# Row scales of the layer norm for two row tiles at a time, and a new order of instructions, in a linear attention and SwiGLU kernel

## The chip, the cores and the metric

The kernel runs on one core of a Trainium2 chip. The metric is the time of one execution on the device in microseconds (us); smaller is better. Engines are named as the profile names them: PE (matmul), PEld (its weight loads), DVE, ACT, POOL, and SP, which here only issues DMAs.

## The reference, cut to what matters

Two kinds of block alternate, twice: linear attention with 32 heads of 16, then a gated MLP. Each reads a layer norm of the running rows and is added to them. There are 2048 rows of 512 numbers, in float32; the MLP's hidden size is 1792. The second attention and the second MLP use the same weights as the first.

```python
def _layernorm(x, axis=-1, eps=1e-5):
    m = jnp.mean(x, axis=axis, keepdims=True)
    v = jnp.var(x, axis=axis, keepdims=True)
    return (x - m) / jnp.sqrt(v + eps)
...
x = x + _A_ref(_layernorm(x, axis=-1), A_wqkv, A_wo)
x = x + _B_ref(_layernorm(x, axis=-1), B_w1, B_w3, B_w2)
x = x + _A_ref(_layernorm(x, axis=-1), A_wqkv, A_wo)
x = x + _B_ref(_layernorm(x, axis=-1), B_w1, B_w3, B_w2)
```

In the attention q and k go through phi(t) = t + 1 or exp(t), plus 1e-6. The sums over all rows of k times v and of k are formed, q is multiplied with the first and divided by its product with the second, and the result goes through wo. The MLP is silu(x w1) times (x w3), times w2.

## The kernel before, in words

The 2048 rows are 16 row tiles of 128, which stay in SBUF as `x_sb`. Every matmul operand is a pair of float16 parts, high and low, and a product is three passes (high by high, low by high, high by low), which `mm` (line 565) issues. In the second layer's keys and queries and in both MLPs, products of two by two blocks are made with seven block products in place of eight, so that many small adds, casts and subtractions (lines 444, 442, 460, 458, 468) surround the matmuls.

For the layer norm of an attention's input, `ln_moments` makes mean and variance of a tile on DVE (BN_STATS and BN_AGGR, lines 526 and 527), and `ln_scale` makes from them the row scale and the row bias on POOL, in four instructions (lines 534, 535, 537, 538): variance plus epsilon, its power of minus one half, minus the mean, and the product of these. `ln_stats(t0, n)` calls both for the n tiles from t0 on; `ln_scale` makes one set of four instructions whatever n is, on n columns. `normalise` (lines 547 and 549) then applies scale and bias to a tile. The MLP's layer norm has code of its own (lines 1458 to 1477), which works on four tiles at a time.

A row tile of keys takes this way in the first layer: statistics, `normalise`, a cast to the high part and a subtraction for the low part (lines 442 or 444, and 468), a transposing DMA (line 1227), twelve matmuls with the key weights (line 565), phi on ACT and DVE (lines 948, 949, 950, 959), a split into high and low (lines 450 and 1048), and the products of the tile with itself that form the sums (line 980). The key weights `wk_s` have to be scaled and split first: four maxima over the weights (line 352), one maximum over them (368), a small matmul (371), a second maximum (373), some arithmetic on single columns (374, 376, 360, 384, 395), four scalings (450, 452) and four subtractions (400).

The first three tiles do not wait for that. `first_tile` normalises them, PE transposes them in float32 (line 1326, four instructions a tile), ACT or DVE copies the result out of the bank (1338, 1340), and `whole_product` multiplies them in float32 with the weights as they were loaded (line 1349, four instructions a tile). A float32 matmul stands in the trace as two. `keep_busy` issues matmuls of a constant tile `ones16` (line 1895; the constant is set by line 268); their results are not used. 19 of them come ahead of everything else in the code, and four behind the first three tiles.

None of this fixes the order in which an engine runs its instructions. `pin_all` does, from the table `ORDER`: one list of places per engine, where place k is the k-th instruction of that engine in the order of the code. `CHOICE` is a string of letters that gives, for each cast, add, scaling or normalisation of which several engines are capable, the engine: V for DVE, P for POOL, A for ACT. `BANKS` gives the PSUM bank of each product. The framework adds the semaphores that the data need. An engine thus runs its list strictly in order, and an instruction that waits holds up all that stands behind it on that engine.

Of the kernel before, what the change touches and what calls it, by code (L numbers as in the profile page):

```python
# [20 lines left out]
NT, NC, NK, NF = S // P, S // 512, D // P, F // P  # L21
# [62 lines left out]
def kernel(  # L84
# [321 lines left out]
    def table_of(what, layer):  # L406
# [3 lines left out]
        "VAPAAPPPAAAAVAPPVAAAPVAAPVAAPPAVPPVAAPAPAVAAAPAPPVVPAPPAAPVAAPAVPPPAVVAPVAAVAVAVAPPAAVAAAVPP"  # L410
        "VVVAPAAAVAAVVAAVAAVVVVAPAVVVAVVAVAVVVPAPAVAPAVPPPAPAVPPVVVPVAVVVAPVAVVAVVPPVAVAVAAPVAPAVAAVV"
        "PPPAVAAAVPVVPPAVAPAVAPAPAPAAAAAPVVVVAVAAPVPPAAAAAAPAPAPAPPVPVAVAPAVAVAAAAAVPPVPVVPPAAPVVPAAV"
        "VAVAVPAPPVAVPPVVAVAVPVAVAAAAAVAVPVVVAVAVVVVVAVAAVAVAAVVVPPAVPVVVVPAVAAVVVVAAVAVVVVVAVAVAVPAP"
        "VVPPVVVVAAPVAAAPAVAVAVVVVVAVAAVVVVVVVAAPPPVAAAVAPPVVAPPVAAAPVPPPPAVAAVPPPAAPVPVAVAAPPAVVVVVV"
        "AAAVVAVVPPVAVVVVVVAVVPVAAVVAAAVPPPPVVVVPVAVAAAAVVVVVAPVVAAVPVAVVPVVAVVVAAPAPVVVPVAAAVVVVVAVA"
        "PAAAAVVVVVVVAAAPVPVVPVVVPVVAAVVAPVAVAPVPVVAVPVAVAAAVVAPVPPVAVPVAAVVVVVVVAVAAAVVAPVPPVAVVVVVV"
        "AAAVVVVVVAVVVVVAAVPPPVVVVAVPVAVAAVAPAAVVVVPPVVVVVPPVVAVAPAVPPAPPPVPAVAPAAAVPAPVVPVAVPVAPPVPV"
        "VVVVVVVAVVVVPVVVAAAVPAPPPPPAVPPAAAAAVVVVVAVVPPVAVAPAVVPAAAAVPAPVVPPVVPVPVPVAVAAAAVPVVVVVAPAV"
        "APPAVPAVVVPVAVAAAVVAVPVVVAVPPVAVAAPPPPPAPVAAVPVAVPPPPAAPPVPPAVAAAVAAAVPPVPPPPPAVAAAAAAAAVAAV"
        "VPVPPVAAAVAAAVVVVPVVPPVVAVAAVAAPPVPVVPPVAVVAVAAVAAPAAVPVVVVVAAAAAVAVAAAVAAAVAAVAPVVVVAAVAPVP"  # L420
        "VPPAVPAVVAAAPAVVVVAAAAVAVPAVAAAAVAPVVVVAAAVAPAVVPVVVAPPAPVAAVAPAVAAVVVVPAPVAAAAAVAVVVPAPVAVA"
        "AAAAVPVVVAVVAAVAVVVVVAVAAAVPPVVVVAVAPPPVPAAPVVPPVVVAVPVAAAAAVPPPPAVVAVVAAAPVPPVVVVVAAAAVVVVV"
        "VVVVAPVVVAAVVVAVPPVAVVPAAAAVVVVVVVVAAPVAAAVVVVVVVVVVAAAVVVVVVVVAAPPVVAAPPAAVPVPVAPVAAAAAVVVV"
        "VVVVAVVAAVPPVVVVVVPAAVAVVVVVVPVAVVAAAAVVVVVVVVAAVVAAAVVPVPVVVVAAAAAVPVVVVVAVAAVVPVVVAVVAAAVV"
        "VVPVVVVAVVAAPPVVPVVVVVAAAVAPVVVVVVAAAAVVVVVVVVVAAVVVVVVVVVAAVVAAVVVVVVVVVVAAAVVVVVVVAVAAAVAP"
        "PVVVVVAAAAAVPVVVVVAAVVAAAVVPVVVVVVAAAAVVVVVVVVAAAVAVAVVVPV"
# [91 lines left out]
    def ln_stats(t0, n):  # L518

        ln_moments(t0, n)  # L520
        ln_scale(t0, n)

    def ln_moments(t0, n):
        for t in range(t0, t0 + n):
            st = small("st", 6)
            nc.vector.bn_stats(st, x_sb[:, t, :])
            nc.vector.bn_aggr(mv_all[:, t, :], st)
# [436 lines left out]
    def attention(layer, ready, prep, before_gram):  # L964
# [24 lines left out]
        for t in range(NT):  # L989
# [919 lines left out]
    ln_stats(1, 1)  # L1909
# [9 lines left out]
    ln_stats(2, 1)  # L1919
# [32 lines left out]
def pin_all(nc, tc):  # L1952
# [5 lines left out]
    for engine, runs in ORDER.items():  # L1958
# [370 lines left out]
```

## Time and profile before

| | us |
|---|---|
| median of three runs | 1141.81 |
| lowest and highest | 1139.44, 1142.08 |
| profiled execution, its time | 1141.3 |
| profiled execution, its span | 1139.5 |
| PE busy in the span | 1125.7 (99%) |
| DVE busy | 974.0 (85%) |
| ACT busy | 595.8 (52%) |
| POOL busy | 390.6 (34%) |

Times in views of the profile count from the start of the span. [...] The group name `arena` stands for nearly everything that lies in SBUF, as it is one tile with many views; lines tell the groups apart. The engine DVE has two instructions for some lines (one reads an accumulator).

### The profile page before, as it was taken

The numbers are of one execution on the slowest core, as the hardware profiler recorded it, in microseconds if no ns is written. First come the engines' busy times: TensorE is split into PE (matmuls) and PEld (weight loads), VectorE is DVE, ScalarE is ACT, GpSimd is POOL, SyncE is SP. The second block draws the span as 40 slices with busy tenths as digits, with TensorE's granted clock in tenths as the row PEclk, the third lists the DMA queues.
The fourth block names the chain that finished last, engine by engine and source line by source line (L and its number), as shares of the span: only waits on it lengthen the run. The fifth ranks groups of instructions, "written<-read, shape, count | busy, mean of one in ns | idle before, by whom it ended". The sixth has DMA issues, their size and how long they took to land.

```text
span 1139.5 us, 22555 instructions
## 1 busy us (share of the span) xinstructions
PE 1125.7 (99%) x9075; PEld 889.3 (78%) x9075; DVE 974.0 (85%) x1705; ACT 595.8 (52%) x1051; POOL 390.6 (34%) x458
## 2 busy tenths in 40 slices
PE   9999999999999999999999999999999999999998
PEld 4445445888888888888876676678888888888887
DVE  7787999999999999898899779989788766777767
ACT  5588778874555245435467657766433233222421
POOL 5750467333550442325688212444300100100000
PEclk9999999999999999999999999999999999999999
DMA  9997467677555232412567646646543613002012
GB/s 279 276 273 252 117 137 196 157 236 225 183 187 230 84 149 103 158 66 70 145 162 208 154 135 186 111 83 172 161 114 130 244 57 122 2 1 75 10 38 93
DMA packets 174298, 164.66 MB, mean 145 GB/s; under 512 B 138864, under 2 KB 150256, under 8 KB 169328
## 3 DMA queue, kind: packets, MB, share of 16 engines
q1 hardware_dynamic: 174192, 163.21, 48.4%
q8 instruction: 71, 1.16, 0.4%
q14 instruction: 35, 0.29, 0.1%
HBM read 80.87 MB, written 48.50 MB: 114 GB/s over the span
## 4 chain that ended last, share of the span: by engine, by line
PE 85%; DVE 8%; DMA 3%; POOL 2%; issue 1%; ACT 1%; SPq 0%; POOLq 0%; DVEq 0%; ACTq 0%
PE bank L565 59%; PE bank L1602 18%; PE bank L980 6%; DVE arena L468 4%; DMA arena<-arena 2%; POOL arena L468 1%; DMA arena<-in_B_w_dram 1%; DVE arena L1560 1%; DVE arena L1650 1%; DVE arena L1510 1%; PE bank L1895 1%; DVE arena L444 1%; POOL rs_all L535 0%; PE bank L1349 0%; POOL arena L460 0%
## 5 line engine op out<-in xcount | busy, mean ns | idle before, releaser
L565 PE MATMUL bank<-arena 128*128 128x256 f16 (+2 forms) x6228 | 804.7, 285 | 8.2 <-DMA arena<-arena 6.7
L565 PEld LDWEIGHTS <-arena 128*128 128x128 f16 x6228 | 605.1, 98 | 169.8 <-DMA arena<-arena 8.8
L468 POOL TENSOR_TENSOR arena<-arena 128x256 f32<-128x256 f32 (+5 forms) x251 | 285.8, 1152 | 633.7 <-DVE arena L1510 158.1
L468 DVE TENSOR_TENSOR arena<-arena 128x256 f32<-128x256 f32 (+4 forms) x555 | 390.4, 730 | 17.6 <-ACT arena L442 6.7
L1602 PE MATMUL bank<-arena 128*128 128x256 f16 x2310 | 291.6, 273 | 0.0
L1602 PEld LDWEIGHTS <-arena 128*128 128x128 f16 x2310 | 226.0, 98 | 26.4 <-ACT arena L442 0.2
L1555 ACT ACTIVATE arena<-bank 128x512 f32<-128x512 f32 x168 | 99.6, 594 | 227.8 <-PE bank L565 189.0
L442 ACT ACTIVATE arena<-arena 128x512 f16<-128x512 f32 (+3 forms) x203 | 153.0, 771 | 66.1 <-DVE arena L468 32.9
L1560 DVE TENSOR_TENSOR arena<-arena,bank 128x512 f32<-128x512 f32 x168 | 113.9, 682 | 39.5 <-ACT arena L1555 22.7
L1650 DVE SCALAR_TENSOR_TENSOR arena<-bank,scalars,arena 128x256 f32<-128x256 f32 (+1 forms) x200 | 111.2, 584 | 25.4 <-PE bank L1602 16.9
L1509 ACT ACTIVATE arena<-arena,scalars 128x512 f32<-128x512 f32 (+1 forms) x112 | 74.4, 666 | 95.2 <-DVE arena L1560 78.8
L1510 DVE SCALAR_TENSOR_TENSOR arena<-arena,scalars 128x512 f32<-128x512 f32 (+1 forms) x112 | 79.6, 713 | 21.7 <-ACT arena L1509 21.2
L980 PE MATMUL bank<-arena 128*128 128x512 f16 (+1 forms) x384 | 91.5, 379 | 0.3 <-DVE arena L1048 0.3
L980 PEld LDWEIGHTS <-arena 128*128 128x128 f16 (+1 forms) x384 | 38.8, 101 | 35.8 <-issue 0.6
L444 DVE CAST arena<-arena 128x512 f16<-128x512 f32 (+2 forms) x82 | 50.5, 619 | 5.5 <-POOL arena L460 1.8
L444 POOL CAST arena<-arena 128x512 f16<-128x512 f32 (+2 forms) x31 | 23.3, 753 | 81.8 <-DVE arena L1089 28.3
L547 ACT ACTIVATE arena<-arena,nb_all,rs_all 128x512 f32<-128x512 f32 x42 | 33.6, 807 | 8.1 <-DVE arena L468 6.5
L1652 ACT ACTIVATE arena<-bank,scalars 128x256 f32<-128x256 f32 x40 | 18.7, 468 | 32.6 <-PE bank L1602 20.2
L458 ACT ACTIVATE arena<-arena,scalars 128x512 f32<-128x512 f32 (+3 forms) x33 | 31.4, 956 | 7.2 <-DMA arena<-in_B_w_dram 4.2
L1048 DVE SCALAR_TENSOR_TENSOR arena<-arena,scalars 128x512 f16<-128x512 f32 x32 | 26.7, 834 | 5.3 <-ACT arena L450 5.0
L1292 ACT ACTIVATE arena<-bank 128x256 f32<-128x256 f32 x51 | 18.9, 375 | 17.4 <-PE bank L565 17.2
L450 ACT ACTIVATE arena<-arena,scalars 128x512 f16<-128x512 f32 x27 | 19.4, 720 | 13.8 <-DVE arena L959 13.4
(117 smaller groups left out, 626.1 us busy)
## 6 DMA issues: line engine op xcount, KB each, us to landing
arena<-xb_d SPq DMA_DIRECT2D x12, 1792.0 KB, 7.0
xb_d<-arena SPq DMA_DIRECT2D x8, 1792.0 KB, 7.2
w_d<-arena SPq DMA_DIRECT2D x5, 1792.0 KB, 7.5
arena<-w_d SPq DMA_DIRECT2D x5, 1792.0 KB, 10.2
arena<-in_B_w_dram SPq DMA_DIRECT2D x8, 896.0 KB, 6.3
arena<-in_B_w_dram SPq DMA_DIRECT2D x28, 256.0 KB, 3.1
xt_d<-arena SPq DMA_DIRECT2D x8, 896.0 KB, 4.3
arena<-xt_d SPq DMA_DIRECT2D x8, 896.0 KB, 5.0
```

The source lines that it names most:

```text
L442: engine.activation(dst, src, AF.Copy)
L444: engine.tensor_copy(dst, src)
L468: choose().tensor_tensor(dst, a, b, op)
L547: engine.activation(dst, x, AF.Identity, scale=scale, bias=bias)
L565: nc.tensor.matmul(dst, lhs(a, k), rhs(b, k), start=first and k == 0 and i == 0, stop=last and k == n - 1 and i == len(PASSES) - 1, skip_g ...
L980: nc.tensor.matmul(gt[j][:n], nat[:, first : first + n], pk[:, b, :], start=t == 0 and i == 0, stop=t == NT - 1 and i == len(PASSES) - 1, ...
L1509: nc.scalar.activation(t, gate, AF.Silu, scale=info["u1"])
L1510: nc.vector.scalar_tensor_tensor(t, up, info["hid"], t, OP.mult, OP.mult)
L1555: engine.activation(dst, bank_, AF.Copy)
L1560: nc.vector.tensor_tensor(dst, dst, bank_, OP.add)
L1602: nc.tensor.matmul(po[:, i * HALF : (i + 1) * HALF], hs[:, a, qx, cs], w2[:, b, qw, :], start=g == ends[0] and i + a + b == 0, stop=g == e ...
L1650: nc.vector.scalar_tensor_tensor(dst, src, cb, to, OP.mult, OP.add)
```

## The change

In the first layer's keys, statistics were made for tile t+4 at each tile t; now they are made for tiles t+4 and t+5 at each even t. In the second layer it was one call for each tile (two at t = 0); now it is one call for two tiles at t = 0 and at each odd t. Ahead of the loop tiles 1 and 2 share one call. The calls of `ln_scale` go from 29 to 16, so that 52 instructions on POOL are left out; 13 of the 16 sets that are left are two columns wide, two are one wide and one is four wide. BN_STATS and BN_AGGR stay one per tile.

```diff
@@ stats() in attention()
                 if layer == 1:
                     if t == 0:
-                        ln_stats(4, 1)
-                        ln_stats(5, 1)
-                    elif t + 5 < NT:
-                        ln_stats(t + 5, 1)
-                elif t + 4 < NT:
-                    ln_stats(t + 4, 1)
+                        ln_stats(4, 2)
+                    elif t % 2 and t + 5 < NT:
+                        ln_stats(t + 5, 2)
+                elif t % 2 == 0 and t + 4 < NT:
+                    ln_stats(t + 4, 2)
@@ ahead of the first layer
     whole_product(0)
-    ln_stats(1, 1)
+    ln_stats(1, 2)
...
     for _ in scale_chain:
         pass
-    ln_stats(2, 1)
     keep_busy(4)
@@ ORDER (one line of the five lists)
-        "0-13 19-22 14-17 23-26 35 18 27-30 40-43 36 31-34 44-47 37 51-53 38-39 48-50 54-56 72-83 "
...
```

`CHOICE` is a new string too. Counted over the whole program, 78 instructions go from POOL to DVE and 46 from DVE to POOL, 41 from ACT to DVE and 24 from DVE to ACT, 19 from ACT to POOL and 17 from POOL to ACT. With the 52 that are left out, the lists of instructions change from 1675 to 1724 on DVE, from 1004 to 985 on ACT and from 463 to 381 on POOL; PE keeps its 9034 matmuls and SP its DMAs, in new orders. From about the middle of the second layer's keys to the end of its attention, PE's list is nearly that of before.

The three places below are all at the start of the program. In the new file the same code stands one line higher from line 1045 on and two lines higher at the end. On PE, before; line 1895 is a matmul of the constant tile, and there are 14 of them ahead of the first row of line 1326, four, one, and one in the gaps that follow; banks 65, 67 and 70 take the transposed tiles 0, 1 and 2, banks 66, 68 and 71 their products:

```order
L2325 UNCONDITIONAL_BRANCH
L1895 LDWEIGHTS ones_76
L1895 MATMUL bank_64<-ones_76 128x512
...
L1326 MATMUL bank_65<-arena 128x128 x4
...
L1349 MATMUL bank_66<-arena 128x512 x4
L371 MATMUL bank_69<-arena,scalars 128x128
...
L1326 MATMUL bank_67<-arena 128x128 x4
L1326 MATMUL bank_70<-arena 128x128 x4
...
L1349 MATMUL bank_68<-arena 128x512 x4
L1349 MATMUL bank_71<-arena 128x512 x4
```

And on PE now, with three matmuls of line 1894 ahead of line 371, then six, seven and four in the gaps:

```order
L2319 UNCONDITIONAL_BRANCH
L1325 MATMUL bank_65<-arena 128x128 x4
L1348 MATMUL bank_66<-arena 128x512 x4
L1894 LDWEIGHTS ones_76
L1894 MATMUL bank_64<-ones_76 128x512
...
L371 MATMUL bank_69<-arena,scalars 128x128
...
L1325 MATMUL bank_67<-arena 128x128 x4
...
L1325 MATMUL bank_70<-arena 128x128 x4
...
L1348 MATMUL bank_68<-arena 128x512 x4
L1348 MATMUL bank_71<-arena 128x512 x4
```

All 14 matmuls of the constant that stood ahead of the first tile now stand behind its product, and 20 of them stand between the products of tile 0 and tile 1.

On DVE, before, from the first instruction on; line 268 sets the constant tile, line 549 normalises tile 0, line 352 takes the maxima of the key weights:

```order
L268 MEMSET ones_76 128x128
L526 BN_STATS arena<-arena 128x6
L527 BN_AGGR mv_all<-arena 128x2
L549 TENSOR_SCALAR arena<-arena,rs_all,nb_all 128x512
...
L352 TENSOR_REDUCE arena<-arena 128x1 x3
...
L368 TENSOR_REDUCE scalars<-arena 128x1
...
L373 TENSOR_REDUCE scalars<-bank_69 128x1
```

And on DVE now:

```order
L526 BN_STATS arena<-arena 128x6
L527 BN_AGGR mv_all<-arena 128x2
L549 TENSOR_SCALAR arena<-arena,rs_all,nb_all 128x512
L352 TENSOR_REDUCE arena<-arena 128x1 x4
...
L368 TENSOR_REDUCE scalars<-arena 128x1
...
L268 MEMSET ones_76 128x128
L1339 CAST arena<-bank_65 128x512
...
L373 TENSOR_REDUCE scalars<-bank_69 128x1
```

The constant is set behind the four maxima and the statistics of tiles 1 and 2, not first of all.

On POOL, before, from the scales of tiles 1 and 2 to their normalisation (line 549); line 558 sets single columns to one:

```order
L534 TENSOR_SCALAR arena<-mv_all 128x1 x2
L535 TENSOR_TENSOR rs_all<-arena,minus_half 128x1
L537 TENSOR_SCALAR arena<-mv_all 128x1
L538 TENSOR_TENSOR nb_all<-arena,rs_all 128x1
L549 TENSOR_SCALAR arena<-arena,rs_all,nb_all 128x512
L558 MEMSET arena 128x1
L535 TENSOR_TENSOR rs_all<-arena,minus_half 128x1
L537 TENSOR_SCALAR arena<-mv_all 128x1
L558 MEMSET arena 128x1
L538 TENSOR_TENSOR nb_all<-arena,rs_all 128x1
L549 TENSOR_SCALAR arena<-arena,rs_all,nb_all 128x512
```

And on POOL now:

```order
L537 TENSOR_SCALAR arena<-mv_all 128x2
L534 TENSOR_SCALAR arena<-mv_all 128x2
L444 CAST arena<-arena 128x512
L535 TENSOR_TENSOR rs_all<-arena,minus_half 128x2
L538 TENSOR_TENSOR nb_all<-arena,rs_all 128x2
L558 MEMSET arena 128x1
L549 TENSOR_SCALAR arena<-arena,rs_all,nb_all 128x512 x2
```

Eight instructions on one column have become four on two columns, tile 1 is normalised only when the statistics of tile 2 are there too, and a cast of tile 0 stands between. On SP the loads of tiles 1 and 2 have moved from the third and fourth place of the queue to the seventh and eighth, behind the key weights and one other row tile.

More of the change, by code (lines that the diff above doesn't have):

```diff
@@ L415 @@
[L415 to L424, printed above, removed]
@@ L425 @@
-        "VVPVVVVAVVAAPPVVPVVVVVAAAVAPVVVVVVAAAAVVVVVVVVVAAVVVVVVVVVAAVVAAVVVVVVVVVVAAAVVVVVVVAVAAAVAP"
-        "PVVVVVAAAAAVPVVVVVAAVVAAAVVPVVVVVVAAAAVVVVVVVVAAAVAVAVVVPV"
+        "VPPAVPAPAVAAAPPVPAAAVVAVAVAAVVAAPVAVAPAAAVVPAVVPPPVAAPAAAPAAAVAPAVPAAVAAPAPVAVPVPPPAPPVAAVPA"
+        "VPVPPAAAVAVVVVAVVVVVVVVVAVVVVVVAVAVVVPAPAVAPAVPVPAPAVPPVVVVVVVAVAVVAVVAVVPPVAVAVAAPVAPAVAAVP"
+        "PPPAVAAAVPVVPPAVAPAVAPAPAPAAAAAVVVPVAVAAPVPPAAAAPAPAPPPAPPVPVAPAVAVAPAAAAAVVPPVAVPPVPPPVPAAV"
+        "VAAAVVAVPVAVPPVVAVAVPPAPAAAAAVAVPVVVAVAVVVVVAVAPVAAAAVVVVVAVAPVVVPAVAAVVVVAAVAVVPVPAVAAAVPAP"
@@ new lines @@
+        "VPPVAVPVAAVVAAAVAVPPAVVPVVAVAAVPVVVVVVAPVVVAAAVAPAVVAPVVAAAAVVPPPAVAAVPPVAAPVPVAVAAPPAVVVVVV"
+        "AVAVVAVVVPVAVVVVVVAVVPVAAVVAAAVPPPPVVVVPVAVAAAAVVVVVAPVVAAVPVAPVPVVAVVVAAPAPVVVPVAAVVVVVVAVA"
+        "PAAAAVVPVVAVAAAPPVVVPVVVPVVAAVVAPVAVVVVPVVAVPVAVAAAVVAPVPPPAVPVAAVAVVVVVAVAAAVVAPVPPVAVVPPVV"
+        "AAAVVVVVVAVVVVVAAVPAPVVVVAVVVAVAAVAPAAVVVVVPVVVVVPPVVAVAPAVPVAPVPVPPVAPAVAVPAVVVVVAVVVAPVVPV"
+        "VVVVVVVAVVVVVVVVAAAVPAPVPPPAVPPAAVAAVVVVVAVVPVVAVAPAVVVAAAAVVAPVVPPVVPVPVPVVPAAAAVPVPVVVPPPV"
@@ new lines @@
+        "AVPAVVAVVVPVAVAAAVVAVPVVVPVPPVAVAAPPPPPAPAAAVPPAVVPVPAAPPPPPAVAAAVAAAAVAAVPPPPAVAAAAAAVAVAAV"
+        "VPVVPVVAAAAAVVVVPPVVVPVVAAAAVAAPVVAVVPVVAVVAVAAVAAVAAVPVVVVPAAAAAAAAAAAVAAAVAAVAAVVVVAAVAPVP"
+        "VPPAVPAVVAAAPAVPVVAAAAVAVPAVAAAAVAPVVVVAAAVAVAVVPVVVAPPAPVAAVAPAVAAVVVVPAPVAAAAAVAVVVPAPVVVA"
+        "AAAAVVVVVAVAAAVAVVVVVAVAAAVPPVVVPAVAAPPVPAAPVVAPVVVAVPVAAAAPVPPVVAVVAVVAAVVVVVVVVVVAVAAVVVVV"
+        "VVVPAPVVVAAVVVAVVPVAVVPAAAAVVVVVVVVAAVVAVAVVVVVVVVVVAAAVVVVVPVVAAPPVPAAVPAVVVVPVAVVAVAAAVVVV"
@@ L427 @@
+        "VVVVAVVAAVPVVPVVVVVAAVAAVVVVVVVVVVAAAAVPVVVVVVVAVVAAAVVPVVAVVVAAAAAPPVVVVVAVAAVVVVVVAVVAAVVV"
+        "VVVVVVVAVVAAVPVVVVVVVVAVAVPVVVVVVVVVAAVVVVVVVVVAAVVVVPVVVVAAVVVAVVVVVVVVVPAAAVVVPVVVVVAAAVAP"
+        "PVVVVVAAAVAVVVVVVVAAVVAAAVVVVVAPVVAAAAVVVVVVVVAVAVAVAVVVPV"
     )
```

5 lines of the change are left out of this document (removed), and 613 rows, old and new, of the table ORDER.

## The prediction

> **What bounds the kernel now.** The first part of the page names the engine that is never idle. The columns are busy time, share of the span, and instructions.
>
> ```profile
> span 1139.5 us, 22555 instructions
> PE 1125.7 (99%) x9075; PEld 889.3 (78%) x9075; DVE 974.0 (85%) x1705; ACT 595.8 (52%) x1051; POOL 390.6 (34%) x458
> ```
>
> PE is idle for 1139.5 − 1125.7 = 13.8 us. An order that leaves PE's matmuls as they are can win those, and what a low clock costs, and no more. The waits of PE, the second view (line waited for, total us, times, longest), say who holds it.
>
> ```profile
> PE bank L565 <- DMA arena<-arena: 6.7, 4, 2.4
> PE bank L1895 <- DVE ones L268: 1.1, 1, 1.1
> PE bank L565 <- ACT arena L1555: 1.0, 2, 0.7
> PE bank L565 <- DVE arena L1650: 0.4, 1, 0.4
> PE bank L980 <- DVE arena L1048: 0.3, 1, 0.3
> ```
>
> Most of it is four waits for a DMA that carries a transposed tile. The timeline of PE (start, length, what, and in brackets the idle time ahead and its releaser) has three of them:
>
> ```profile
> 25.26 2.76 PE L565 MATMUL bank<-arena 128*128 128x512 f16 x12 [0.66 <-DMA arena<-arena]
> 30.26 4.45 PE L565 MATMUL bank<-arena 128*128 128x512 f16 x12 [2.23 <-DMA arena<-arena]
> 34.55 4.05 PE L980 MATMUL bank<-arena 128*128 128x512 f16 x18
> 182.75 3.65 PE L565 MATMUL bank<-arena 128*128 128x512 f16 x28
> 188.78 3.42 PE L565 MATMUL bank<-arena 128*128 128x512 f16 x18 [2.38 <-DMA arena<-arena]
> ```
>
> The first two are the key products of tiles 3 and 4 in the first layer. The third is in that attention's output. A transposing DMA only carries what DVE, ACT or POOL made, so I read in the windows who was busy ahead of each (columns PE, PEld, DVE, ACT, POOL, PEclk, DMA share, GB/s):
>
> ```profile
> 0.00:30.00 30.00, 25.97 (x94) 12.45 (x94) 22.95 (x60) 15.69 (x25) 17.32 (x52) 1.00 0.91 285
> 30.00:60.00 30.00, 29.74 (x131) 13.60 (x132) 23.58 (x35) 17.03 (x27) 22.78 (x47) 0.94 0.96 271
> 60.00:90.00 30.00, 29.90 (x141) 13.97 (x140) 25.63 (x36) 26.12 (x49) 13.06 (x14) 1.00 0.87 259
> 90.00:120.00 30.00, 30.00 (x181) 16.20 (x179) 24.10 (x65) 25.72 (x57) 1.16 (x1) 1.00 0.63 220
> 120.00:150.00 30.00, 30.00 (x141) 13.52 (x140) 28.87 (x58) 21.55 (x47) 19.63 (x19) 1.00 0.53 140
> 150.00:180.00 30.00, 30.00 (x142) 13.78 (x141) 29.07 (x51) 23.05 (x48) 21.50 (x22) 1.00 0.66 133
> 180.00:210.00 30.00, 27.62 (x190) 18.30 (x189) 29.71 (x64) 27.13 (x57) 16.64 (x16) 1.00 0.68 188
> ```
>
> Ahead of the wait at 188.78 DVE is full: from 120 to 180 it is idle for 1.13 + 0.93 = 2.06 us only. From 30 to 120 it has 6.42 + 4.37 + 5.90 = 16.7 us to spare. So the program has two places at which an order decides, the first 35 us and the stretch up to 189 us. Elsewhere PE has its work ready.
>
> The profiled run took 1141.3 us, 1.8 more than its span; the median is 1141.81, so what I reckon against the profile stands 0.5 below the median. A difference under 0.3%, 3.4 us, can't be told from no change here.
>
> **The four instructions on POOL.** The groups of POOL by form (total us, mean ns):
>
> ```profile
> L535 POOL TENSOR_TENSOR rs_all<-arena,minus_half 128x1 f32<-128x1 f32 x28 | 18.6, 691 | 0.7
> L535 POOL TENSOR_TENSOR rs_all<-arena,minus_half 128x4 f32<-128x4 f32 x1 | 1.0, 1038 | 0.0
> L534 POOL TENSOR_SCALAR arena<-mv_all 128x1 f32<-128x1 f32 x28 | 13.0, 463 | 8.1 <-DVE mv_all L527 6.3
> L537 POOL TENSOR_SCALAR arena<-mv_all 128x1 f32<-128x1 f32 x28 | 10.2, 368 | 2.8 <-DVE mv_all L527 1.7
> L538 POOL TENSOR_TENSOR nb_all<-arena,rs_all 128x1 f32<-128x1 f32 x28 | 8.2, 299 | 0.6
> ```
>
> One set is 691 + 463 + 368 + 299 = 1821 ns. Thirteen sets fall away: 23.7 us. A two-column power isn't in the trace; between one column (691) and four (1038) I take 691 + 347/3 = 807, so 13 wider sets give back 1.5 us. Net, POOL loses 22 us. POOL is busy for a third of the span, so nearly all of that is time in which it waited. It reaches PE in one place, the chain ahead of the wait of 0.4 us on line 1650:
>
> ```profile
> 563.94 1.62 POOL rs_all L535 x2
> 566.82 1.31 POOL arena L534
> 576.02 0.82 PE bank L565 x6
> ```
>
> Here two separate power instructions are one, 0.8 us sooner, and the wait is 0.4 at most. I take −0.2 (0 to −0.4).
>
> **The start: PE.** PE's first rows before:
>
> ```profile
> 1.10 5.88 PE L1895 MATMUL bank<-ones 128*128 128x512 f16 x14 [1.10 <-DVE ones L268]
> 6.82 1.05 PE L1326 MATMUL bank<-arena 128*128 128x128 f32 x8
> 8.57 3.69 PE L1349 MATMUL bank<-arena 128*128 128x512 f32 x8
> 12.53 1.95 PE L1326 MATMUL bank<-arena 128*128 128x128 f32 x16
> 14.31 0.38 PE L1895 MATMUL bank<-ones 128*128 128x512 f16 x1
> 14.53 7.03 PE L1349 MATMUL bank<-arena 128*128 128x512 f32 x16
> 21.40 0.38 PE L1895 MATMUL bank<-ones 128*128 128x512 f16 x1
> ```
>
> Between a tile's transposes and its product stands the copy out of the bank, here on ACT:
>
> ```profile
> 13.62 0.60 ACT L1338 ACTIVATE arena<-bank 128x512 f32<-128x512 f32 x1 [4.11 <-PE bank L1326]
> ```
>
> The constant's 14 matmuls cost 5.88/14 = 0.42 us each; the later one at 14.31 makes room in 0.22. So the clock was half for about 5.6 us from PE's first matmul on, whatever PEclk says, and then whole. These 14 lie beside the load and the statistics of tile 0 and cost nothing; tile 0 itself ran at the whole clock (3.69 us for eight records). Now they stand behind tile 0, which therefore is PE's first work and runs cold: its transposes from 6.8 take 2 × 1.05 = 2.1, to 8.9; the copy takes 0.6, and the product starts at about 9.6. If the clock again rises 5.6 us after the first matmul, at 12.4, then 2.8 us pass cold (3.3 records of 0.86) and the other 4.7 take 0.43 each: the end is 14.4, where it was 8.57 + 3.69 = 12.26. Twenty matmuls of the constant, the small one of line 371 and sixteen transposes follow: 4.3 + 0.2 + 1.8 = 6.3; the products of tiles 1 and 2 take 21.40 − 14.53 = 6.87. That ends at 27.6, where it was 21.4. Nine matmuls of line 980 and three of the constant (2.6) bring 30.2, two warm key products (24 × 0.216 = 5.2) bring 35.4. The same point before was 34.55. So PE's own list is 0.85 late.
>
> [...]
>
> **The start: DVE.** The key products need the scaled weights, and their scale passes through lines 371 and 373 on DVE:
>
> ```profile
> 12.52 0.29 DVE L373 TENSOR_REDUCE scalars<-bank 128x1 f32<-128x128 f32 x1 [0.68 <-PE bank L371]
> 24.70 2.44 DVE L400 SCALAR_TENSOR_TENSOR arena<-arena,scalars 128x512 f16<-128x512 f32 x3
> ```
>
> Line 371 now follows the cold product and three constants (0.65), and before, line 373 started 0.43 after line 371 (next rows: 12.52, and 12.09 in the same timeline): it starts at 14.4 + 0.65 + 0.43 = 15.5 and ends at 15.8. From there to the last of the four subtractions of line 400 stand 44 instructions on DVE. At the window's mean of 22.95/60 = 0.383 us that is 16.8, so 32.6; before, it was 24.70 + 2.44 = 27.14. So DVE is 5.5 late and PE has to wait for it, for 32.6 − 30.2 = 2.4 us. The rest of tile 3's product (0.9) and tile 4's (2.6) end at 36.1: +1.5 against 34.55. Bounds: if the clock is whole at once, the product ends at 12.0, all is 2.4 sooner, and DVE's path gives 33.7, −0.8; if the whole product runs cold it ends at 16.5, +3.6. With the nearest row being the 5.6 us, I take +1.5.
>
> The two loads that moved back in SP's queue don't count. Nine loads of this kind show this row (KB each, median us to landing):
>
> ```profile
> arena<-in_A_x_dram SPq DMA_DIRECT2D x9, 256.0 KB, 5.3
> ```
>
> Issued in the seventh and eighth place, about half a microsecond apart, they land near 9.4. That leaves 7 us for one set of scales (1.8) and two tiles' statistics and normalisation until PE transposes tile 1 at about 17.
>
> **From 30 to 120 us.** DVE comes out of the start 5.5 late, PE 1.5. Up to the next key product, 8 us on, DVE can win back 8.2 × 6.42/30 = 1.75 of the 4.0 between them; 2.25 are left. How far ahead of PE a tile stood there no row shows, so the cost is between 0 and 2.25; I take the middle, +1.1. PE is then 2.6 late.
>
> **Up to 189 us.** The tile at 188.78 hangs on DVE. Matched instruction by instruction, 299 DVE instructions stood ahead of its last addition and now 314 do, 15 more; some nine of them come before the place that DVE had reached at 120, six behind it. Nine, at 974.0/1705 = 0.571, are 5.1 us, which with the 4.0 of lag fit into 16.7 us of idle time. Six are 3.4, less 2.06 idle, 1.4. So DVE is later than before by 1.4 (if its idle time had let it catch up with the old times) to 1.4 + 2.6 = 4.0 (if it follows PE); I take the middle, 2.7. PE has 1.3 us of matmuls more ahead of the wait. PE was ready at 186.40; now at 186.40 + 2.6 + 1.3 = 190.3, the tile at 188.78 + 2.7 = 191.5. PE waits 1.2 and, its 1.3 us of work brought forward, goes on 2.7 − 1.3 = 1.4 late. The place gives back 2.6 − 1.4: −1.2. Bounds: −2.4, all of the wait, to +4.7 (all 15 instructions on the path, 8.6 less 1.3 less the lateness of 2.6).
>
> Behind that, PE's order is nearly the old one, up to the same place of the second layer; I cost it at nothing, as PE's backlog hides it (the window of 90 to 120 shows PE without a gap).
>
> **Sum**: 1.5 + 1.1 − 1.2 − 0.2 = +1.2. On 1141.3 that is 1142.5.
>
> **Rivals.** *DVE is the bound up to 189 us.* All 15 instructions count, since 1.16 us of POOL and 24.1 of DVE in 90 to 120 may mean that DVE waits on data there and can't run ahead. DVE is 8.6 late, PE 1.3 richer: +7.3, −0.2: **1148.4**. It decides from the point where DVE is over 4.0 late at 189. For it speaks that the 41 instructions from ACT come to an engine at 97% there; against it the 16.7 us to spare.
>
> *PE finds everything ready: faster.* [...] The lines of one operation, as lowest, median and highest ns:
>
> ```profile
> L1048 DVE SCALAR_TENSOR_TENSOR arena<-arena,scalars x32: 719/750/1671, 21.4 to 659.5; 128x512 f16<-128x512 f32 x32
> ```
>
> The same subtraction takes 719 or more than double; something at times holds it up. If the 44 instructions took 14.4 us and not 16.8, and the clock rose early, the start would be bound by PE's list: 0.85 − 2.4 = −1.5. The wait at 188.78 (2.38) and that at 576 (0.4) would go: −4.3, **1137.0**. It decides from the point where DVE's path is shorter than PE's list, 2.4 us at the start. Against it: a median 4% above the lowest leaves little to win.
>
> [...]
>
> *The change does nothing that shows*: the start's lateness only eats up the wait at 188.78, of which 2.6 − 2.4 = 0.2 is left, less 0.2: **1141.3**.
>
> **How the numbers follow.** The forecast has a chance of 0.38, its own range is 1141.0 to 1146.0; of it 0.33 lie within 0.3% of the median (up to 1145.2), 0.05 above. The rival with nothing to show has 0.12. The faster one has 0.26, of which 0.24 under 1138.4; the slower 0.24. Together: faster 0.24, same 0.33 + 0.12 + 0.02 = 0.47, slower 0.05 + 0.24 = 0.29. The range reaches to both outer rivals, 1136.8 to 1149.0, and leaves about one in ten beyond each.
>
> **What would show it.** Right: tile 0's product ends near 14.4 and its matmuls stand 0.43 apart first; line 373 starts near 15.5; the last line 400 ends near 33; the first matmul of line 980 behind two key products starts near 36.1; the wait at about 190 is about 1 us. Wrong: tile 0's product ends near 12 or the last line 400 before 30 (faster), or a wait of over 4 us near 195 (slower), or new waits for a DMA between 200 and 1100 us, of which this sum has none.

## The result and the profile after

| | before | after |
|---|---|---|
| median (us) | 1140.91 of four runs | 1148.99 of four runs |
| lowest and highest | 1139.44, 1142.08 | 1147.69, 1150.37 |
| profiled execution: span | 1139.5 | 1146.4 |

The ratio is 1.0073, with a 95% interval of 1.0058 to 1.0088: slower by about 8 us. The forecast was 1142.5, no change that can be told; the time is that of the slower rival (1148.4), but, as will be seen, not by its mechanism. One execution of e16 below took 3065 us and is left out of that run's ratio.

The page of the changed kernel, first lines:

```profile
span 1146.4 us, 22505 instructions
PE 1127.1 (98%) x9075; PEld 888.5 (78%) x9075; DVE 990.4 (86%) x1754; ACT 584.5 (51%) x1032; POOL 344.0 (30%) x376
```

PE is idle for 19.3 us, 5.5 more than before. The waits of PE:

```profile
PE bank L1325 <- DVE arena L549: 6.6, 1, 6.6
PE bank L565 <- DMA arena<-arena: 4.3, 6, 1.1
PE bank L565 <- ACT arena L1554: 1.1, 1, 1.1
PE bank L980 <- DVE arena L1047: 0.9, 3, 0.4
PE bank L1348 <- ACT arena L1337: 0.7, 1, 0.7
PE bank L371 <- DVE arena L959: 0.5, 1, 0.5
```

A reader could stop at the first line: PE now waits 6.6 us for tile 0 where it waited 1.1 for the constant, and the difference is all of the new idle time. But the 14 matmuls that lay in that stretch before did no work for the result, so this line says where the constant went and not where the time went. For that one follows PE from landmark to landmark. The timeline of PE in the changed kernel:

```profile
6.57 2.07 PE L1325 MATMUL bank<-arena 128*128 128x128 f32 x8 [6.57 <-DVE arena L549]
9.33 6.42 PE L1348 MATMUL bank<-arena 128*128 128x512 f32 x8 [0.69 <-ACT arena L1337]
15.59 0.81 PE L1894 MATMUL bank<-ones 128*128 128x512 f16 x3
...
21.91 7.03 PE L1348 MATMUL bank<-arena 128*128 128x512 f32 x16
...
32.01 5.43 PE L565 MATMUL bank<-arena 128*128 128x512 f16 x24
37.28 2.11 PE L980 MATMUL bank<-arena 128*128 128x512 f16 x9
39.22 2.75 PE L565 MATMUL bank<-arena 128*128 128x512 f16 x12
41.81 0.60 PE L980 MATMUL bank<-arena 128*128 128x512 f16 x2
42.76 2.96 PE L980 MATMUL bank<-arena 128*128 128x512 f16 x13 [0.36 <-DVE arena L1047]
46.87 2.76 PE L565 MATMUL bank<-arena 128*128 128x512 f16 x12 [1.14 <-DMA arena<-arena]
49.48 7.29 PE L980 MATMUL bank<-arena 128*128 128x512 f16 x33
```

The records of PE overlap (a float16 matmul of line 980 or 565 stands as 0.38 us long, and the next starts 0.216 us behind it), so the end of tile 4's key product is told by the start of the row behind it: 37.28, where it was 34.55, 2.7 us late. Further on (line 371 belongs to the background work on the next weights):

```profile
63.36 0.49 PE L371 MATMUL bank<-arena,scalars 128*128 128x128 f32 x2 [0.55 <-DVE arena L959]
...
65.42 2.77 PE L565 MATMUL bank<-arena 128*128 128x512 f16 x12 [0.93 <-DMA arena<-arena]
...
87.95 2.76 PE L565 MATMUL bank<-arena 128*128 128x512 f16 x12 [0.34 <-DMA arena<-arena]
...
116.73 0.95 PE L1101 MATMUL bank<-scalars,arena 128*128 128x1 f32 x8
...
196.09 23.89 PE L565 MATMUL bank<-arena 128*128 128x512 f16 x168 [0.94 <-DMA arena<-arena]
...
231.35 3.87 PE L565 MATMUL bank<-arena 128*128 128x256 f16 x34 [1.12 <-ACT arena L1554]
...
1136.96 5.40 PE L1621 MATMUL bank<-arena 128*128 128x256 f16 x48
```

and the same two landmarks, the end of the keys and the last products, in the kernel before:

```profile
109.96 0.95 PE L1102 MATMUL bank<-scalars,arena 128*128 128x1 f32 x8
...
1129.97 5.40 PE L1622 MATMUL bank<-arena 128*128 128x256 f16 x48
```

At the end of the first layer's keys PE is 116.73 − 109.96 = 6.8 us late; at the last products 7.0. So in these two executions 2.7 us were lost by the end of tile 4, 4.1 between there and 110 us, and nearly nothing in the thousand microseconds behind. One execution is a small sample here: the same place, the end of tile 4's product, came at 34.55 in this execution of the kernel before, but at 30.84 in e9 and 31.16 in e5, which run the same order up to there.

### The profile page after: what moved, and what is told of

Its sections match the earlier page's. It is cut to its first block, busy times and chain, and to the rows that moved or that the text cites. A ratio compares the mean times of both kernels' runs of the same rounds, so it can differ in the third digit from the quotient of the medians.

```text
span 1146.4 us, 22505 instructions
## 1 busy us (share of the span) xinstructions
PE 1127.1 (98%) x9075; PEld 888.5 (78%) x9075; DVE 990.4 (86%) x1754; ACT 584.5 (51%) x1032; POOL 344.0 (30%) x376
## 4 chain that ended last, share of the span: by engine, by line
PE 83%; DVE 8%; DMA 4%; issue 2%; ACT 2%; POOL 1%; SPq 0%; DVEq 0%; POOLq 0%; ACTq 0%
PE bank L565 58%; PE bank L1601 19%; PE bank L980 5%; DVE arena L468 3%; DMA arena<-arena 2%; DVE arena L1649 1%; DVE arena L1509 1%; DMA arena<-in_B_w_dram 1%; DVE arena L1559 1%; DMA arena<-in_A_wqkv_dram 1%; PE bank L1348 1%; POOL arena L468 1%; DVE arena L526 0%; ACT arena L450 0%; POOL rs_all L535 0%
## 5 line engine op out<-in xcount | busy, mean ns | idle before, releaser
L468 POOL TENSOR_TENSOR arena<-arena 128x256 f32<-128x256 f32 (+5 forms) x225 | 263.4, 1186 | 684.6 <-DVE arena L468 225.5
L468 DVE TENSOR_TENSOR arena<-arena 128x256 f32<-128x256 f32 (+5 forms) x581 | 400.2, 717 | 15.0 <-ACT arena L442 9.3
L1554 ACT ACTIVATE arena<-bank 128x512 f32<-128x512 f32 x157 | 92.7, 592 | 188.7 <-PE bank L565 155.9
L444 DVE CAST arena<-arena 128x512 f16<-128x512 f32 (+3 forms) x89 | 53.9, 609 | 3.9 <-DMA arena<-arena 1.2
L444 POOL CAST arena<-arena 128x512 f16<-128x512 f32 (+3 forms) x28 | 19.4, 697 | 50.4 <-PE bank L565 11.4
L1556 DVE COPY arena<-bank 128x512 f32<-128x512 f32 x39 | 26.8, 687 | 8.7 <-PE bank L565 8.0
L458 ACT ACTIVATE arena<-arena,scalars 128x1024 f32<-128x1024 f32 (+2 forms) x29 | 29.2, 1011 | 5.2 <-POOL arena L468 3.0
```

Of the source, the lines that this page charges most:

```text
L444: engine.tensor_copy(dst, src)
L468: choose().tensor_tensor(dst, a, b, op)
L1554: engine.activation(dst, bank_, AF.Copy)
```

## Experiments

Each was compared with runs of the kernel before on the same chip; "us" is the ratio's distance from 1 times that median. Three theories stood at the outset. Start: everything follows from tile 0 being PE's first, cold work (its product took 6.42 us, 3.69 before) with 14 matmuls of the constant behind it. Order: the new order from 37 us on makes waits of its own. Pair: a tile waits for its partner's statistics. Line numbers in the rows of a run are those of its own file, which are a few off from run to run.

| run | median | ratio, interval | us |
|---|---|---|---|
| changed kernel | 1148.99 | 1.0073, 1.0058 to 1.0088 | +8.3 |
| e1 | 1145.0 | 1.0041, 1.0027 to 1.0056 | +4.7 |
| e2 | 1146.95 | 1.0061, 1.0044 to 1.0079 | +7.0 |
| e3 | 1155.72 | 1.0137, 1.0119 to 1.0156 | +15.6 |
| e4 | 1142.43 | 1.0021, 1.0010 to 1.0032 | +2.4 |
| e5 | 1139.83 | 0.9999, 0.9988 to 1.0010 | −0.1 |
| e6 | 1150.24 | 1.0090, 1.0074 to 1.0105 | +10.3 |
| e7 | 1144.28 | 1.0040, 1.0025 to 1.0055 | +4.6 |
| e8 | 1138.27 | 0.9986, 0.9975 to 0.9997 | −1.6 |
| e9 | 1142.94 | 1.0039, 1.0026 to 1.0053 | +4.4 |
| e10 | 1143.54 | 1.0040, 1.0028 to 1.0053 | +4.6 |
| e11 | 1152.86 | 1.0125, 1.0111 to 1.0139 | +14.2 |
| e12 | 1150.62 | 1.0102, 1.0088 to 1.0116 | +11.6 |
| e13 | 1141.62 | 1.0012, 1.0001 to 1.0024 | +1.4 |
| e14 | 1147.35 | 1.0061, 1.0047 to 1.0075 | +7.0 |
| e15 | 1142.85 | 1.0018, 1.0008 to 1.0029 | +2.1 |
| e16 | 1141.65 | 1.0010, 1.0000 to 1.0020 | +1.1 |

**e1: the constants first again.** In the changed kernel, PE's list gets its old beginning (numbers are places in the order of the code; 0 to 18 are the constants, 19 to 26 tile 0), and line 268 goes to the head of DVE's list:

```diff
-        "19-26 0-2 35 3-8 27-30 9-15 40-43 16-18 36 31-34 44-47 37 51-53 38-39 57-59 54-56 72-83 "
+        "0-13 19-22 14-17 23-26 35 18 27-30 40-43 36 31-34 44-47 37 51-53 38-39 57-59 54-56 72-83 "
```

> The changed kernel, but PE's first 51 matmuls and the setting of the constant stand as before: 14 matmuls of the constant ahead of tile 0. Everything else is the changed order. Start theory (the whole loss follows from tile 0's cold product and the 14 matmuls behind it, and the waits from 42 to 88 us are its knock-on): about 7 us less than the changed kernel, near 1142. Order theory (the start costs its 2.7 us, and the waits from 42 to 88 us belong to the new order there): 2.7 less, near 1146, with those waits still there. Pair theory (tiles wait for the partner's statistics): near 1146 too.

About half of the loss went (3.6 of 8.3). PE now waits 1.60 us at 14.07 for line 549 on POOL, the normalisation of tiles 1 and 2, which share one set in the new order. Then it runs into the next limit, a wait for the high part of a tile's keys on ACT, behind which the matmuls run at half rate again (six take 2.57 us, where 1.46 is usual) until the products of tiles 3 and 4 have begun. The view ends at 34 us, inside its last row:

```profile
26.09 0.59 PE L980 MATMUL bank<-arena 128*128 128x512 f16 x2 [2.68 <-ACT arena L450]
...
27.52 2.57 PE L980 MATMUL bank<-arena 128*128 128x512 f16 x6
29.89 4.45 PE L565 MATMUL bank<-arena 128*128 128x512 f16 x17
```

The waits at 60, 62 and 85 us stayed (0.51, 0.84, 0.77). That speaks against start alone.

**e2: the mirror, in the kernel before.**

```diff
-        "0-13 19-22 14-17 23-26 35 18 27-30 40-43 36 31-34 44-47 37 51-53 38-39 48-50 54-56 72-83 "
+        "19-26 0-2 35 3-8 27-30 9-15 40-43 16-18 36 31-34 44-47 37 51-53 38-39 48-50 54-56 72-83 "
```

> The kernel before, but PE's first 51 matmuls stand as in the changed kernel (tile 0 first, the 14 matmuls of the constant behind it), and the constant is set behind the maxima. Start theory: about 7 us more than before, near 1148, with new waits for transposed tiles between 35 and 90 us. Order theory and pair theory: 2 to 3 more, near 1144, and no such waits. If the old order's own waits at 25 and 30 us take up the lateness, less than 2 more.

It cost 7.0, as the start theory had it, with new waits for transposed tiles (0.91 us at 55.84, 0.69 at 66.30); its profiled execution, the fastest of six runs, shows a span only 2.6 longer. By e2 alone the start would be nearly everything, by e1 it is half. Together (4.7 left, 7.0 made) they come to more than the loss, so the two parts overlap, and cuts in time were needed (e5, e6, e9, e10).

**e3: single sets in the new order.**

```diff
-                elif t % 2 == 0 and t + 4 < NT:
-                    ln_stats(t + 4, 2)
+                elif t + 4 < NT:
+                    ln_stats(t + 4, 1)
```

(and so in the second layer and ahead of the loop).

> The changed kernel's order and engines, but every set of row scales is made for one tile again: each of the 13 double sets becomes two, side by side on POOL. Start and order theory: within 1 us of the changed kernel, as POOL has time to spare. Pair theory: also near it while the statistics stand in pairs; a few tenths of a us either way tell what the 52 instructions are worth.

All theories missed: 7.3 us worse than the changed kernel. Its longest new wait, with a slow product behind it (4.45 us for its twelve matmuls, 2.75 to 2.77 in most rows):

```profile
61.02 4.45 PE L565 MATMUL bank<-arena 128*128 128x512 f16 x12 [3.35 <-DMA arena<-arena]
```

So in the new order the 52 instructions do not fall into spare time on POOL: the merged sets are worth about 7 us to it. Which of POOL's other steps they delay was not followed further.

**e4: double sets alone, in the old order.** The edit of e3 the other way round; on POOL the set of a pair stands at its first tile's place, on DVE the second tile's statistics stand right behind the first's.

> The kernel before in its own order, with the 13 double sets alone: the set of a pair stands where the first of its two stood, and the statistics of the second tile behind those of the first. Start and order theory: within 1 us of before, near 1141.5. Pair theory: 3 to 7 more, near 1146, with waits between 40 and 90 us.

2.4 more (1.1 to 3.7), which neither theory had, and next to none of it between 40 and 90 us (one wait of 0.49 at 59.28). Its new waits lie at the second layer's beginning (560 to 604 us; before, there was 0.4 us):

```profile
559.86 1.80 PE L1601 MATMUL bank<-arena 128*128 128x256 f16 x15 [1.28 <-DVE arena L1559]
...
592.45 0.82 PE L565 MATMUL bank<-arena 128*128 128x256 f16 x6 [0.92 <-DVE arena L1293]
...
598.70 0.82 PE L565 MATMUL bank<-arena 128*128 128x256 f16 x6 [0.81 <-DVE arena L1649]
...
600.81 1.02 PE L980 MATMUL bank<-arena 128*128 128x512 f16 x4 [0.87 <-DVE arena L1047]
```

In the old order the pair theory falls for the first layer. (In the new order a pair can hold PE up at the start, as line 549 does in e1 and e16, for 1.60 and 1.45 us.) The change in the code, without a new order, is a small loss.

**e5 and e6: a cut at 95 us.** Both are made of the two orders, for all engines at once: what had started by the cut in one trace in that kernel's order, the rest in the other's. The code is that of the old sets on one side and of the double ones on the other, as for e5:

```diff
                 if layer == 1:
                     if t == 0:
-                        ln_stats(4, 1)
-                        ln_stats(5, 1)
-                    elif t + 5 < NT:
-                        ln_stats(t + 5, 1)
+                        ln_stats(4, 2)
+                    elif t % 2 and t + 5 < NT:
+                        ln_stats(t + 5, 2)
```

> On every engine the order, the engines and the single sets of before for all that had started by 95 us in its trace; behind that the changed kernel's order, engines and double sets. Early theory (the whole loss is made in the first 95 us, by the start and by the new order there): the same as before, 1139 to 1141. Late theory (the new order's own waits behind 200 us, on lines 1554, 1509 and 1649, add to it): 3 to 4 more than before, near 1144.

> The mirror: the changed kernel's order, engines and double sets for all that had started by 102 us in its trace, then the order of before with single sets. Early theory: the changed kernel's time, 1147 to 1149. Late theory: 3 to 4 less than the changed kernel, near 1145.

Clear: with the old first 95 us the new order is the time of before (−0.1), with the new first 95 us the old order is the changed kernel's or more (+10.3, whose interval overlaps that of +8.3). The loss is made in the first 95 us. The late waits of the new order (1.12 at 231 us) stand against those that it lacks (1.43 at 734 us in the kernel before).

**e7: 14 constants left out** of the changed kernel.

```diff
-    keep_busy(19)
+    keep_busy(5)
```

> The changed kernel without 14 of the matmuls of the constant (those that stand ahead of line 371 and of the transposes of tiles 1 and 2). If PE's own list holds the start, as its trace says (no wait ahead of the key products of tiles 3 and 4): 14 x 0.216 = 3.0 less, near 1146. If the scaled key weights hold it: at most 1 less, with a wait for a DMA ahead of tile 3's product in place of the constants. If the clock falls again without them, more than now.

8.3 became 4.6. PE's own list did hold the start, but with the constants gone PE waits 2.31 us for line 450 at 27.20. The key products of tiles 3 and 4 end at 35.19, 2.1 sooner, and 1.2 of these are tile 0's product, which ended at 14.51 and not at 15.75, as it took 5.45 us in this execution and not 6.42. So the traces show less than 1 us for the constants at this place; the rest of the gain stands in the medians only.

**e8: constants in the gap of the kernel before.**

```diff
+                if t == 4:
+                    for _ in range(9):
+                        nc.tensor.matmul(
+                            pp.rearrange("p (a n) -> p a n", a=4),
+                            ones16,
+                            ones16[:, None, :].to_broadcast([P, 4, P]),
+                            start=True,
+                            stop=True,
+                        )
                 if t not in whole:
                     mm(
```

In PE's list they stand just ahead of tile 4's product.

> The kernel before, with nine more matmuls of the constant (into the bank of the product that follows) in PE's gap of 2.23 us ahead of tile 4's key product at 30 us. If it is the gap that lowers the clock for the next 4 us: tile 4's product takes 2.8 and not 4.45 us, and the total is 1.7 less, near 1138.5, unless the wait at 189 us takes it back, as nothing else changed there: then the same as before.

The product takes 2.76 us at the place where it took 4.45, and the kernel is 1.6 us (0.3 to 2.8) faster than before:

```profile
27.95 2.10 PE L999 MATMUL bank<-ones 128*128 128x512 f16 x9
30.00 2.76 PE L565 MATMUL bank<-arena 128*128 128x512 f16 x12
32.60 4.05 PE L980 MATMUL bank<-arena 128*128 128x512 f16 x18
```

32.60 against 34.55 is 1.95 us at that place. They do not last: PE waits 1.42 us at 62.22 and 0.87 at 86 us, where it did not wait before, and the product behind the wait at 189 us starts at the same time in both traces (188.81 and 188.78). So in these two traces the filled gap keeps the rate up, but where the 1.6 us of the medians come from is not shown; e8's trace gains behind 189 us, about half of it in a wait at 734 us (0.23 for 1.43). Nor is the gap in every execution. Tile 4's transposing DMA took 5.8 us before and 5.5 in e8; in e5 and e9, with the same order there, it took 4.2, and PE went from tile 3's product to tile 4's without a gap.

**e9 and e10: a cut at 35 us.** As e5 and e6, with double or single sets split at tile 8:

```diff
-                elif t + 4 < NT:
+                elif t + 4 < NT and not (t + 4 >= 8):
                     ln_stats(t + 4, 1)
+                elif t % 2 == 0 and t + 4 < NT:
+                    ln_stats(t + 4, 2)
```

> On every engine the order of before for what had started by 35 us in its trace (single sets for the tiles up to 7), then the changed order with double sets. Knock-on theory (the waits from 42 to 88 us of the changed kernel only pass on what its first 37 us were late on DVE, ACT and the DMA queue): the same as before, near 1140. Own-order theory (the order from 37 to 95 us makes them itself): 3 to 5 more, near 1144, with waits ahead of line 371 and of key products from 40 to 90 us.

> The mirror: the changed order for what had started by 37.5 us in the changed kernel's trace (double sets for the tiles up to 7), then the order of before with single sets. Knock-on theory: 7 to 10 more than before, near 1149, with waits from 40 to 90 us. Own-order theory: what the start itself costs, 3 to 5 more, near 1144.

Two halves that add up: 4.4 and 4.6 make 9.0, against 8.3. The knock-on theory falls. The waits ahead of line 371 that the own-order theory expected did not come in e9; the second half shows in one place, undisturbed by a late start:

```profile
30.84 2.10 PE L980 MATMUL bank<-arena 128*128 128x512 f16 x9
33.13 2.77 PE L565 MATMUL bank<-arena 128*128 128x512 f16 x12 [0.19 <-DMA arena<-arena]
35.74 3.40 PE L980 MATMUL bank<-arena 128*128 128x512 f16 x15
42.67 2.77 PE L565 MATMUL bank<-arena 128*128 128x512 f16 x12 [3.53 <-DMA arena<-arena]
```

The product at 42.67 is tile 6's. In the kernel before the same product came later in PE's list:

```profile
38.44 2.75 PE L565 MATMUL bank<-arena 128*128 128x512 f16 x12
41.02 5.99 PE L980 MATMUL bank<-arena 128*128 128x512 f16 x27
46.85 2.75 PE L565 MATMUL bank<-arena 128*128 128x512 f16 x12
```

Count line 980 ahead of it: 9 + 18 + 27 = 54 matmuls before, 9 + 9 + 15 = 33 now. The tile isn't late: its DMA landed at 42.62, at 43.10 before, and at 42.41 in e5, which has the old order there, ended tile 4's product within 0.3 us of e9 and came to tile 6 at 43.47 without a wait. In e9 PE comes to it 21 matmuls, 4.5 us, too early, while 33 of them stand behind it.

**e11 and e12: SP's old order up to 95 us**, in the changed kernel and in e1:

```diff
-        "0 2 11 5 4 3 1 6 9 34 10 46 7-8 25 24 12 30 40 52 47 55 13 19 44 51 22 20 23 48 29 35 27-28 "
+        "0 2 1 6 4 3 5 7 47 9 24 11 10 25 48 8 12 30 44 51-52 13 29 19 35 20 22 40 23 55 34 27 62 "
```

> The changed kernel, but SP issues the DMAs that had started by 95 us before in the order of before. Queue theory (loads and transposes stand late in the changed queue; the DMA share is 0.70 in the first 30 us where it was 0.91, and 1.04 from 60 to 90): 2 to 4 less than the changed kernel, near 1146. If the queue only follows the engines: within 1 of the changed kernel, or more, as the old queue waits for other tiles first.

> The kernel with the old start on PE (the first experiment, 1145.0) and with SP's old order up to 95 us as well. Queue theory: the waits at 60, 62 and 85 us go, 2 to 3 less than the first experiment, near 1142.5. Otherwise near 1145 with a wait of over 2 us on line 450 near 26 us as there, which neither the start of PE nor the queue then explains.

Both are worse, by 6 and 7 us, e12 by more than either theory had. The old queue doesn't fit the new lists of the engines, and going back to it wins nothing; the queue theory falls.

**e13 and e14: 21 products of line 980 back ahead of tile 6** (whose product has the places 132 to 143), on PE alone, in e9 and in the changed kernel:

```diff
-        "96-107 48-50 60-62 66-68 120-131 84-86 63-65 87-89 69-71 90-92 132-143 93-95 117-119 111-116 "
-        "108-110 153-155 150-152 144-149 168-170 177-179 156-167 171-176 201-203 192-194 228 195-197 "
+        "96-107 48-50 60-62 66-68 120-131 84-86 63-65 87-89 69-71 90-95 117-119 111-116 108-110 "
+        "153-155 147-149 132-143 150-152 144-146 168-170 177-179 156-167 171-176 201-203 192-194 "
```

> The kernel with the old order up to 35 us and the new order behind (1142.9), with one move on PE: 21 products of line 980 stand ahead of tile 6's key product again, as before. PE-order theory (the tile is no later than before, PE only comes to it with too little work ahead): the wait of 3.5 us for it goes, 3 to 4 less, the time of before. If the other engines' order there makes the loss: the products moved ahead wait for line 1049 or 450 instead, and less than 1 us is won.

> The changed kernel with the same single move of 21 products of line 980 ahead of tile 6's key product. PE-order theory: the waits of 0.36 and 1.14 us there go, 1 to 1.5 less than the changed kernel, near 1147.5, and no more, as PE comes 4 us later to this place here than in the other kernel, so that the tile is nearly ready. If the later waits at 63, 65 and 88 us take that up: the same as the changed kernel.

e9's 4.4 became 1.4, and the changed kernel's 8.3 became 7.0, both as the PE-order theory has it, though the second lies inside the intervals. In e13 the moved products and tile 6 run without a gap, where 3.53 us stood:

```profile
36.24 7.93 PE L980 MATMUL bank<-arena 128*128 128x512 f16 x36
44.01 2.75 PE L565 MATMUL bank<-arena 128*128 128x512 f16 x12
```

e13's profiled span (1140.1) is no shorter than e9's (1139.4), as its later waits at 54 to 59 us came up (1.84 together); the gain of 3 us rests on 12 and 5 runs, not on the traces. In e14 tile 6's wait went as well, but PE then waits 1.32 us for tile 7 at 56.16, 1.24 ahead of line 371 at 63.63 and 0.98 for tile 8 at 65.75. So in the changed kernel the tiles behind tile 6 are late too, and the move can win little there.

**e15 and e16: the start taken apart.** e10 without 14 constants (the edit of e7), and e10 with the constants first (the edit of e1).

> The kernel with the new order up to 37 us and the old order behind (1143.5), without 14 matmuls of the constant ahead of the products of tiles 1 and 2. Constants theory (they stand in PE's way at 0.216 each): 3.0 less, near 1140.5, with nearly no new wait before 35 us. Cold-clock theory (tile 0's product and the weights' scale behind it are late): under 1 less, with a wait for line 450 or a DMA between 25 and 35 us in place of the constants.

> The same kernel (1143.5), with PE's first 51 matmuls and the setting of the constant as before: the 14 matmuls warm the clock ahead of tile 0 and cost nothing. Constants theory: the same gain as without them, 3.0. Both together: 4 to 5 less, the time of before. If the new start's order on DVE, ACT and POOL is late by itself: under 3 less, with a wait for line 450 near 26 us, as in the first experiment.

4.6 became 2.1 and 1.1. Neither single cause holds. Without the constants PE meets a wait for ACT; with them first, a wait for POOL and then the same wait for ACT, earlier:

```profile
27.66 0.59 PE L980 MATMUL bank<-arena 128*128 128x512 f16 x2 [2.32 <-ACT arena L450]
```

```profile
13.97 2.05 PE L1328 MATMUL bank<-arena 128*128 128x128 f32 x16 [1.45 <-POOL arena L549]
...
26.00 1.42 PE L980 MATMUL bank<-arena 128*128 128x512 f16 x3 [2.68 <-ACT arena L450]
```

So of the start's 4.6 us some 2.5 went with the constants out of PE's way (e15), another 1 with tile 0's product in 3.69 us, where it took 5.62 in e15, and the weights' scale sooner as well (e16), and about 1 stays with the new order on the other engines, whose waits the rows show. The intervals are about 1.2 us wide to each side, and those of e15 and e16 overlap, so the 1 for the rate could be nothing.

## Why the prediction was wrong

**The start, right in kind, mis-sized (+1.5 for 4.6).** Tile 0 was PE's first work and its product ran slow (6.42 us, 3.69 before), the constants stood in PE's way, and the order of the steps was as forecast. Each came later. The rate doubled not 5.6 us after the first matmul but 8.0 to 8.6, in the seventh of the eight records (the starts of the second to the seventh lie 0.853 us apart, the next two steps are 0.546 and 0.430): the product took 6.42 us and not 4.8, and ended at 15.75, where 14.4 was forecast and 16.5 was the bound. DVE followed from there, in the first and last of these rows 1.2 us late (15.5 and 32.6 forecast):

```profile
16.66 0.29 DVE L373 TENSOR_REDUCE scalars<-bank 128x1 f32<-128x128 f32 x1 [3.35 <-PE bank L371]
...
33.02 0.75 DVE L400 SCALAR_TENSOR_TENSOR arena<-arena,scalars 128x512 f16<-128x512 f32 x1
```

Only the wait for it did not come: PE's own list was as late (32.01 for the 30.2 forecast), and the two products ran through without a gap. The new time was nearly right: 37.28 for the 36.1 forecast in this execution, where tile 0's product took 6.42 us (5.70 in e10), and 36.24 and 36.28 in e6 and e10, which have the same order there. The old time that it was measured against was not. 34.55 holds the gap of 2.23 us and the slow product behind it; with the old order this place came at 30.84 to 31.52 in e9, e5 and e13, about 5 us ahead of e6 and e10. e10 puts the whole start at 4.6.

**From 30 to 120 us, the step that failed (+1.1 for 4.1).** It was costed as DVE's lag out of the start, 0 to 2.25, with the remark that no row shows how far ahead of PE a tile stood. e9 has the old start, hence no such lag, and still loses 4.4: the new order makes the loss itself. For one tile a row did show the lead: tile 6's product follows 27 matmuls of line 980 without a wait, and the new order of PE had 21 of them behind the product. The order was compared on DVE up to 189 us, and on PE only up to the first tiles; the term had no place for work taken away from ahead of a wait. With the 21 back ahead of it, 3.0 of e9's 4.4 go (e13). In the changed kernel, where PE comes to tile 6 later, the same move is worth 1.3, which its interval can't tell from nothing (e14), and the waits at 63 and 65 us stay. What makes those later tiles late was not tested and is open; the chain ahead of the wait at 65.42 runs through DVE, where 2.20 us of maxima of the next weights (line 352) stand from 56.09, and through a transposing DMA that takes 5.24.

**DVE's idle time shows no sign of having absorbed the lag.** The changed kernel's windows:

```profile
30.00:60.00 30.00, 28.43 (x130) 12.83 (x130) 23.80 (x39) 19.65 (x31) 16.77 (x32) 1.00 0.86 245
60.00:90.00 30.00, 28.18 (x131) 12.83 (x130) 23.43 (x33) 22.06 (x39) 18.02 (x16) 1.00 1.04 273
```

6.2 and 6.6 us are idle, where 6.42 and 4.37 were before. It was not free to use: the trace has DVE waiting there, from 30 to 90 us 8.7 us for ACT (4.0 for line 949, 3.3 for 950, 1.4 for 450) and 3.4 for loads.

**The wait at 189 us, right (−1.2).** It fell from 2.38 to 0.94, as PE came later. The size was met in part by luck: the tile itself came 7.3 us later (196.09 for 188.78), where 2.7 was forecast. The slower rival needed over 4 us there, so its number was met by chance; the loss was complete at 110 us. **Behind it, right (0)**: e5 gives −0.1. **POOL's chain at 576 us, right (−0.2)**: the changed kernel's list of waits has none for that line any more. A power of two columns took 846 ns, where 807 was taken:

```profile
L535 POOL TENSOR_TENSOR rs_all<-arena,minus_half 128x2 f32<-128x2 f32 x13 | 10.9, 846 | 0.3
```

**The base was high.** The profiled execution of before (1141.3) stands above the medians of the later sessions (1138.8 to 1140.5), and its gap at 30 us with the slow product behind, 4.1 us together, made the start look cheap: 2.7 late by the two traces at 37 us, 4.6 by the medians of e10.

**The faster rival** needed DVE's path to be shorter than PE's list at the start. That came true, as PE did not wait for DVE there, but only because PE's list itself had become later. Its 14.4 us for the 44 instructions on DVE is not what the changed kernel shows: they took 16.8 (16.95 to 33.77). The subtraction of line 1048 (1047 there) came out no shorter either: lowest, median and highest 732, 748 and 1759 ns, where they were 719, 750 and 1671.

## What to carry to other kernels

Where an order is changed, count for each operand that arrives late how much ready work stands ahead of its first use on the engine that waits, before and after; a tile that is no later than before still made a wait where that work had moved behind it (e9: 3.53 us for tile 6, with 33 products of line 980 ahead of it and not 54). Filler work was free here only where PE would have waited anyway: ahead of tile 0 the 14 constants lay in a wait and took 5.88 us, and tile 0's product behind them 3.69. Moved behind tile 0, they took time of their own (2.5 of e10's 4.6 us went without them, e15), and tile 0's product, now PE's first, took 5.45 to 6.42 us in the changed kernel, e7, e10 and e15 (worth about 1 us by e16, or nothing). Nine more of them in the gap of 2.23 us kept the rate up in e8 (2.76 us for the product that took 4.45), but nothing of the 1.95 us won there was left at 189 us, with new waits of 1.42 and 0.87 us at 62 and 86 us. And look at a place in more than one execution before a forecast is measured against it: 34.55 here was 3 us or more above what the same order gave in e5, e9 and e13.

## What the runs showed of the hardware

How long PE stayed slow at the start differed from run to run. From PE's first matmul at 1.10 the rate doubled after about 5.5 us in the kernel before (starts 0.427 us apart, then 0.216), whose 14 constants took 5.88 us; the same 14, started at the same time, took 4.52 in e1 and 6.09 in e9. With tile 0 first and a pause of 0.69 us in it, tile 0's product alone took 6.42 us in the changed kernel, against 3.69 before, and less in e10 and e15, which start in the same way:

```profile
9.05 5.70 PE L1351 MATMUL bank<-arena 128*128 128x512 f32 x8 [0.69 <-ACT arena L1340]
```

```profile
9.34 5.62 PE L1351 MATMUL bank<-arena 128*128 128x512 f32 x8 [0.69 <-ACT arena L1340]
```

After pauses it was as uneven: 2.23 us of idle time before, 2.68 in e1 and 3.35 in e3 were followed by slow matmuls (4.45 us for twelve, 2.57 for six and 4.45 for twelve), 3.53 in e9 and 2.32 in e15 were not (2.77 for twelve, and 1.46 for the same six of line 980 as in e1). So in these executions a pause of 2.23 us had slow matmuls behind it and one of 3.53 had none; what decides it was not tested. Behind the 2.23 the column for the granted clock shows it too: 0.94 from 30 to 60 us, and 0.50 from 30.5 to 33.8. At the start that column says 1.00 for the first 30 us of either kernel, also from 1.10 to 6.70 before and from 6.50 to 15.60 after, which hold the slow matmuls, so there the rate of the matmuls is the better witness.
